# An adaLN, sliding-attention and SwiGLU kernel: chunk 0's softmax and attention output moved into the projection loop, loads of x and w_mod re-arranged

## The chip, the cores and the metric

The kernel runs on one core of a Trainium2 chip. Its time is the device time of one execution in microseconds. Where a text names an engine: TensorE (PE in the profile, PEld its weight loads), VectorE (DVE), ScalarE (ACT), GpSimd (POOL) and SyncE (SP), which here only issues DMAs.

## The reference

2048 tokens of width 576 (bf16) pass a modulated layer norm, attention of 32 heads of 18 over 8 earlier positions at distance 0, 2, ..., 14, a second modulated layer norm and a SwiGLU of width 4608.

```python
mod = (_silu(c) @ w_mod).reshape(c.shape[0], 6, 1, -1)      # sa, ca, ga, sb, cb, gb
h = _layernorm(x, axis=-1) * (1 + ca) + sa
x = x + ga * _A_ref(h, A_wqkv, A_wo)
h = _layernorm(x, axis=-1) * (1 + cb) + sb
x = x + gb * _B_ref(h, B_w1, B_w3, B_w2)
...
off = jnp.arange(W) * dil                                   # W, dil = 8, 2
idx = pos[:, None] - off[None, :]
mask = idx >= 0
logits = jnp.einsum('bhsd,bhswd->bhsw', q, kg) * scale      # kg = k[idx], vg = v[idx]
logits = jnp.where(mask[None, None, :, :], logits, -1000000000.0)
attn = _softmax(logits, axis=-1)
o = jnp.einsum('bhsw,bhswd->bhsd', attn, vg)                # then @ wo
...
h = _silu(x @ w1) * (x @ w3)                                # then @ w2
```

## The kernel before

Activations are held transposed, features on partitions and tokens in columns, in four chunks of 512 tokens.

**Prologue (L137 to L251).** 16 tiles of x are loaded through three buffers (`xst`, L139), alternately by SP and ACT, transposed on TensorE into `xT` and copied out by VectorE and ScalarE in turn. Then `w_mod` and `c` are loaded by GpSimd (L159 to L170) into a pool (`modp`) opened after `xst` is closed, so that it takes the same space. 150 small matmuls (L189) make the six modulation vectors `modT`. The indicator matrices `ind` and `indT4m` (which sum 18 features to a head, and spread a head's weight over its features) are built here too. `wqkv_sb` is loaded into the space of `modp` when that is released.

**Phase 1 (L280 to L344).** For each chunk n: the layer norm of chunk n+1 (`layer_norm_cols`, L91: statistics by matmuls with ones, then for five feature tiles a triple of VectorE operations: subtract L124, scale L128, shift L133), 75 matmuls for q, k and v (`pp`, L294 and L307, evacuated by ScalarE), and for each of the 8 distances j five products q*k on VectorE (`prod`, L324), five matmuls that sum them to heads (`lp`, L333) and a scaled copy to `lsb` (L339). A DMA puts the chunk's logits into `Lr` as rows 32n to 32n+31 (L342).

**Softmax (L348 to L387).** `Lr` is [128, 8, 512]: four chunks of 32 heads on partitions. One pass over it for all chunks: max over j, subtract, Exp on ScalarE, sum, reciprocal, product to `A_all`.

**Units (`emit_o_units`, L410).** A chunk has 40 units, five feature tiles by 8 distances: a matmul spreads the weights to the features (`aexp_ps`, L418), ScalarE copies them to bf16 (`aexp`, L425), VectorE multiplies with the shifted v (`tj`, L433) and adds to `oT` (L436).

**Head of a chunk (`head_of_chunk`, L444).** Projection by `wo`, gated residual into `xT` (L458), LN2 into `h2T`.

**Sweeps (L470 and L521).** Sweep a: for 36 tiles f of the hidden width load `w1c` and `w3c`, five matmuls for `up` and five for `gate`, a sigmoid on ScalarE, two products on VectorE to `hsw`; the units of the next chunk are spread over its tiles. Sweep b: 36 x 5 matmuls with `w2_sb`, residual, and transposes to the output.

The sequence of the main program is: phase 1 for four chunks, softmax, `w2_sb` load (L395, L396, into the space of the tiles before it), units and head of chunk 0, then for each chunk sweep a, head of the next chunk, sweep b.

A scheduler of the framework simulates the program and sets each engine's queue by program order and readiness; every engine then works through its queue in order. Pools are taken from two ends of the memory (`side="right"` and left) like stacks, so that a tile in re-used space waits for the last users of that space. The number of buffers of a pool sets how far a loop runs ahead.

## Time and profile before

| | us |
|---|---|
| median of 6 runs | 848.15 |
| lowest and highest | 845.93, 850.33 |
| profiled execution | 850.33 |
| its span | 848.5 |
| PE busy | 745.9 (88% of the span) |
| DVE busy | 512.1 (60%) |
| ACT busy | 299.7 (35%) |
| POOL busy | 81.0 (10%) |

The span is what the profiler saw, from the first to the last instruction; 1.8 us of the execution lie outside it. The shares are means over stages that have different limits, so they are read by stretches of time: prologue to about 52 us, phase 1 to 201.6, softmax to 233, units and head of chunk 0 with the first units of chunk 1 to about 296, sweeps to the end. A granted clock of 1.00 is 2.4 GHz, 0.50 is 1.2 GHz.

### The profile page before, as it was taken

The page shows a single profiled execution, that of the slowest core. Times are in us where ns is not written, and L with a number is a line of the kernel's source. Part 1 is how long each engine was busy: PE and PEld are TensorE (multiplying, and loading weights), DVE is VectorE, ACT ScalarE, POOL GpSimd, SP SyncE. Part 2 cuts the span into 40 slices and gives each one's busy share as a digit, 9 for nine tenths or more (in the row PEclk, how much of TensorE's full clock was granted, in tenths as well). Part 3 has the DMA queues.
Part 4 walks back from the last instruction along what each step waited for, and adds up shares of the span by engine and source line. Part 5 has one row for each costly group of instructions (what it writes and reads, how often), then busy time and mean ns, then how long its engine had stood idle before and what let it go on. Part 6 is the DMA issues. An engine that isn't in the chain of part 4 may idle for free.

```text
span 848.5 us, 11370 instructions
## 1 busy us (share of the span) xinstructions
PE 745.9 (88%) x3275; PEld 315.5 (37%) x3275; DVE 512.1 (60%) x1058; ACT 299.7 (35%) x521; POOL 81.0 (10%) x381
## 2 busy tenths in 40 slices
...
GB/s 135 196 103 0 1 25 25 1 25 67 0 250 1 21 95 111 111 89 109 7 76 110 109 112 92 8 29 134 112 108 111 35 15 98 113 112 112 42 1 28
DMA packets 185281, 62.15 MB, mean 73 GB/s; under 512 B 176068, under 2 KB 183428, under 8 KB 185092
## 3 DMA queue, kind: packets, MB, share of 16 engines
...
q10 hardware_dynamic: 91940, 27.10, 13.6%
...
q8 instruction: 26, 0.43, 0.2%
...
## 4 chain that ended last, share of the span: by engine, by line
PE 49%; DVE 12%; issue 9%; ACT 4%; DMA 2%; POOL 0%; ACTq 0%; POOLq 0%; DVEq 0%
PE gate_ps L504 18%; PE up_ps L497 13%; PE out_ps L529 10%; PE aexp_ps L418 3%; PE pp L452 2%; DVE g L512 2%; ACT sig L510 2%; DMA w1c<-in_B_w_dram 1%; DVE t L128 1%; DVE tj L433 1%; DVE t L124 1%; ACT aexp L425 1%; DVE h2T_new L133 1%; DVE oT_next L436 1%; DVE oT_cur L436 1%
## 5 line engine op out<-in xcount | busy, mean ns | idle before, releaser
L504 PE MATMUL gate_ps<-h2T_new,w1c 128*128 128x512 bf16 x720 | 182.4, 380 | 7.7 <-DVE g L512 4.0
L497 PE MATMUL up_ps<-h2T_new,w3c 128*128 128x512 bf16 x720 | 183.9, 382 | 2.9 <-DVE h2T_new L133 2.9
L510 ACT ACTIVATE sig<-gate_ps 128x512 bf16<-128x512 f32 x144 | 86.1, 598 | 263.3 <-PE gate_ps L504 244.8
L529 PE MATMUL out_ps<-hsw,w_sb 128*128 128x512 bf16 (+1 forms) x720 | 173.0, 382 | 6.8 <-DVE xT L535 4.5
L512 DVE TENSOR_TENSOR g<-gate_ps,sig 128x512 bf16<-128x512 f32 x144 | 99.3, 689 | 98.3 <-ACT sig L510 97.8
L425 ACT CAST aexp<-aexp_ps 126x512 bf16<-126x512 f32 (+1 forms) x160 | 88.0, 585 | 68.7 <-PE aexp_ps L418 37.7
L504 PEld LDWEIGHTS <-w1c 128*128 128x128 bf16 x720 | 69.0, 97 | 106.8 <-issue 39.0
L529 PEld LDWEIGHTS <-w_sb 128*128 128x128 bf16 (+1 forms) x720 | 72.1, 101 | 94.1 <-issue 16.0
L515 DVE TENSOR_TENSOR hsw<-g,up_ps 128x512 bf16<-128x512 bf16 x144 | 98.5, 685 | 9.1 <-PE out_ps L529 1.0
L497 PEld LDWEIGHTS <-w3c 128*128 128x128 bf16 x720 | 70.1, 98 | 84.5 <-issue 3.8
L418 PE MATMUL aexp_ps<-A_all,indT4m 128*126 128x512 bf16 (+1 forms) x160 | 60.6, 426 | 42.5 <-DVE A_all L384 31.2
L535 DVE SCALAR_TENSOR_TENSOR xT<-out_ps,modT,xT 128x512 bf16<-128x512 f32 (+1 forms) x20 | 14.9, 747 | 106.5 <-PE out_ps L529 106.5
L324 DVE TENSOR_TENSOR prod<-qT,kT 128x512 bf16<-128x512 bf16 (+11 forms) x160 | 57.1, 414 | 23.0 <-PE lp L333 11.7
L294 PE MATMUL pp<-hT_n,wqkv_sb 128*128 128x512 bf16 (+3 forms) x200 | 58.0, 398 | 4.8 <-DVE hT_n L133 3.6
L433 DVE TENSOR_TENSOR tj<-aexp,vT 126x512 bf16<-126x512 bf16 (+10 forms) x140 | 57.4, 418 | 3.4 <-ACT aexp L425 2.4
L493 POOL MEMSET w3c<- 64x128 bf16 x144 | 28.7, 200 | 262.9 <-PE up_ps L497 233.8
L494 POOL MEMSET w1c<- 64x128 bf16 x144 | 29.6, 206 | 253.6 <-PE gate_ps L504 189.3
L333 PE MATMUL lp<-prod,ind 128*32 128x512 bf16 (+1 forms) x160 | 47.4, 383 | 0.0
L418 PEld LDWEIGHTS <-indT4m 128*126 128x126 bf16 (+1 forms) x160 | 22.7, 144 | 65.9 <-issue 55.7
L436 DVE TENSOR_TENSOR oT_next<-oT_next,tj 126x512 bf16<-126x512 bf16 (+1 forms) x105 | 44.0, 419 | 1.5
L95 ACT ACTIVATE sq_t<-xT 128x512 bf16<-128x512 bf16 (+1 forms) x40 | 24.2, 627 | 32.3 <-PE stat_ps L109 24.4
L294 PEld LDWEIGHTS <-wqkv_sb 128*128 128x128 bf16 (+3 forms) x200 | 17.8, 101 | 45.3 <-issue 37.8
...
## 6 DMA issues: line engine op xcount, KB each, us to landing
...
wmod_sb<-in_w_mod_dram POOLq DMA_DIRECT2D x1, 3456.0 KB, 13.6
...
out_dram<-ob POOLq DMA_DIRECT2D x16, 144.0 KB, 2.3
```

Of the source, the lines that this page charges most:

```text
L294: nc.tensor.matmul(pp[0:orows, :], lhsT=wqkv_sb[0:krows, kc, col0:col0 + orows], rhs=hT_c[0:krows, kc, :], start=(kc == 0), stop=(kc == NS ...
L324: nc.vector.tensor_tensor(out=prod[0:rows, fc, lo:TC], in0=qT[0:rows, fc, s0 + lo:s0 + TC], in1=kT[0:rows, fc, s0 + lo - sh:s0 + TC - sh], ...
L418: nc.tensor.matmul(aexp_ps[0:rows, :], lhsT=indT4m[:, cc, fc, 0:rows], rhs=A_all[:, j, :], start=True, stop=True,)
L425: nc.scalar.copy(aexp[0:rows, :], aexp_ps[0:rows, :])
L433: nc.vector.tensor_tensor(out=tj[0:rows, lo:TC], in0=aexp[0:rows, lo:TC], in1=vsrc, op=ALU.mult)
L436: nc.vector.tensor_tensor(out=oT_c[0:rows, fc, lo:TC], in0=oT_c[0:rows, fc, lo:TC], in1=tj[0:rows, lo:TC], op=ALU.add,)
L497: nc.tensor.matmul(up_ps[:, :], lhsT=w3c[:, kc, :], rhs=h2T_c[:, kc, :], start=(kc == 0), stop=(kc == NSC - 1),)
L504: nc.tensor.matmul(gate_ps[:, :], lhsT=w1c[:, kc, :], rhs=h2T_c[:, kc, :], start=(kc == 0), stop=(kc == NSC - 1),)
L510: nc.scalar.activation(out=sig[:, :], in_=gate_ps[:, :], func=AF.Sigmoid)
L512: nc.vector.tensor_tensor(out=g2[:, :], in0=gate_ps[:, :], in1=sig[:, :], op=ALU.mult)
L515: nc.vector.tensor_tensor(out=hsw[:, f, :], in0=g2[:, :], in1=up_ps[:, :], op=ALU.mult)
L529: nc.tensor.matmul(out_ps[0:orows, :], lhsT=w2_sb[:, f, col0:col0 + orows], rhs=hsw[:, f, :], start=(f == 0), stop=(f == NF - 1),)
```

## The change

1. **Prologue.** `xst` has 16 buffers and SP issues all x loads at the start. The pool of `wmod_sb` and `cT` is opened before that of x, so it has space of its own. The loads of `cT` stand first on GpSimd, before the identity matrix is built. Two one-element copies from the 12th x tile into `wmod_sb` stand before its load, which by that is issued after that tile has landed.
2. **Chunk 0's softmax by itself.** After chunk 0's logits, four DMAs put them in `L0` as [128, 8, 128], four groups of 128 tokens on partitions, and a softmax of a quarter of the width gives `A0`; it is written in phase 1, before chunk 1's part. The big softmax follows after phase 1 as before, for chunks 1 to 3 (rows 0 to 31 of `Lr` are zeros), and its logits are now bf16.
3. **Chunk 0's units in phase 1.** 20 are written into the part of n=2 and 20 into that of n=3, each with four matmuls of 128 columns from `A0` in place of one of 512 from `A_all`.
4. **Buffers.** `p1ps` 4 to 3, `lps` 3 to 2, `hp` 3 to 2, `qT` per chunk (2) in place of whole, `aexp` and `tj` 3 to 2 (pool `ostg`), two PSUM banks for `aexp` during phase 1; later `ps_up` 3 to 2 and `ps_misc` 1 to 2.

TensorE's queue has 240 rows more, 120 matmuls and 120 loads. Between the last `lp` and the second `gate` of the first sweep stand 88 matmuls of units and 28 of projections by `wo` before the change, and 3 and 25 after it. From that gate on stand 2410 matmuls before and 2447 after; 29 of the 37 more are of units.

```diff
+    ostg = ctx.enter_context(tc.tile_pool(name="ostg", bufs=2, side="right"))
+    modp = tc.alloc_tile_pool(name="modp", bufs=1, side="right")
+    wmod_sb = modp.tile([128, NSC, 6 * D], BF16)
+    cT = modp.tile([128, NSC, 1], BF16)
+    for kc in range(NSC):
...
+        nc.gpsimd.dma_start(
+            cT[0:rows, kc, :],
...
+            if cc == 0:
+                for sub in range(NSUB):
+                    nc.tensor.matmul(
+                        aexp_ps[0:rows, sub * SUB:(sub + 1) * SUB],
+                        lhsT=indT4m[:, sub, fc, 0:rows],
+                        rhs=A0[:, j, :],
+                        start=True, stop=True,
+                    )
...
+    def softmax8(Lt, dstA, T, pool):
+        m4 = pool.tile([128, 4, T], F32, tag="m4")
+        nc.vector.tensor_tensor(out=m4[:, :, :], in0=Lt[:, 0:4, :], in1=Lt[:, 4:8, :], op=ALU.max)
...
+        Eb = pool.tile([128, NJ, T], BF16, tag="Eb")
+        nc.scalar.activation(out=Eb[:, :, :], in_=Lt[:, :, :], func=AF.Exp)
...
+        nc.vector.tensor_tensor(
+            out=dstA[:, :, :], in0=Eb[:, :, :],
+            in1=rsum[:, None, :].to_broadcast((128, NJ, T)), op=ALU.mult,
+        )
...
+        ps_aexp = pro.enter_context(tc.tile_pool(name="ps_aexp_pro", bufs=2, space=bass.MemoryType.PSUM))
...
-            xst = p0x.enter_context(tc.tile_pool(name="xst", bufs=3, side="right"))
+            xst = p0x.enter_context(tc.tile_pool(name="xst", bufs=16, side="right"))
...
+            for ti in range(NTOK128):
+                xs = xst.tile([128, D], BF16, tag="xs")
+                nc.sync.dma_start(xs[:, :], x2d[ti * 128:(ti + 1) * 128, :])
+                xs_all.append(xs)
+            nc.gpsimd.tensor_copy(wmod_sb[0:1, 0, 0:1], xs_all[11][0:1, 0:1])
+            nc.gpsimd.tensor_copy(wmod_sb[0:1, 4, 0:1], xs_all[11][0:1, 0:1])
+            nc.gpsimd.dma_start(
+                wmod_sb[:, 0:4, :], w_mod[0:512, :].rearrange("(kc p) o -> p kc o", p=128)
+            )
...
-                DMAQ[ti % 2].dma_start(xs[:, :], x2d[tsl, :])
...
-        Lr = att.tile([128, NJ, TC], F32)
-        hp = tc.alloc_tile_pool(name="hp", bufs=3, side="right")
+        Lr = att.tile([128, NJ, TC], BF16)
+        L0 = att.tile([128, NJ, SUB], BF16)
+        hp = tc.alloc_tile_pool(name="hp", bufs=2, side="right")
...
+        o0_parts = split_units(all_units(), NCH - 2)
...
-            p1ps = pps.enter_context(tc.tile_pool(name="p1ps", bufs=4, space=bass.MemoryType.PSUM))
-            lps = pps.enter_context(tc.tile_pool(name="lps", bufs=3, space=bass.MemoryType.PSUM))
+            p1ps = pps.enter_context(tc.tile_pool(name="p1ps", bufs=3, space=bass.MemoryType.PSUM))
+            lps = pps.enter_context(tc.tile_pool(name="lps", bufs=2, space=bass.MemoryType.PSUM))
...
+                if n >= 2:
+                    emit_o_units(0, oT0, o0_parts[n - 2], ps_aexp)
...
+                if n == 0:
+                    for sub in range(NSUB):
+                        DMAQ[sub % 2].dma_start(
+                            L0[32 * sub:32 * (sub + 1), :, :],
+                            lsb[0:H, :, sub * SUB:(sub + 1) * SUB],
+                        )
...
+                        softmax8(L0, A0, SUB, smp)
+                else:
+                    DMAQ[n % 2].dma_start(
+                        Lr[32 * n:32 * (n + 1), :, :], lsb[0:H, :, :]
+                    )
...
-    aexpp = ctx.enter_context(tc.tile_pool(name="aexpp", bufs=3, side="right"))
-    tjp = ctx.enter_context(tc.tile_pool(name="tjp", bufs=3, side="right"))
...
-    ps_up = ctx.enter_context(tc.tile_pool(name="ps_up", bufs=3, space=bass.MemoryType.PSUM))
+    ps_up = ctx.enter_context(tc.tile_pool(name="ps_up", bufs=2, space=bass.MemoryType.PSUM))
...
-    ps_misc = ctx.enter_context(tc.tile_pool(name="ps_misc", bufs=1, space=bass.MemoryType.PSUM))
+    ps_misc = ctx.enter_context(tc.tile_pool(name="ps_misc", bufs=2, space=bass.MemoryType.PSUM))
...
-    emit_o_units(0, oT_cur, all_units())
+    oT_cur = oT0
```

The first place is GpSimd's queue in the prologue, from the identity matrix to the small loads (`PE_49` and the like are the semaphores waited for; DMAHW ones are completion counters of DMAs). Before:

```order
masks.py:197 MEMSET ident 128x128
L245 MEMSET indT4m 128x2560
masks.py:199 ISA
masks.py:199 AFFINE_SELECT ident<-ident 128x128 [waits Pool_49]
L159 DMA wmod_sb<-in_w_mod_dram 128x4x3456 [waits DMAHW4_49,DMAHW3_49,DMAHW5_49,DMAHW2_49,DMAHW6_49,DMAHW1_49,DMAHW7_49,DMAHW0_49,PE_49]
L162 DMA wmod_sb<-in_w_mod_dram 64x3456
L167 DMA cT<-in_c_dram 128x1 x4
L167 DMA cT<-in_c_dram 64x1
```

After:

```order
L95 DMA cT<-in_c_dram 128x1 x4
L95 DMA cT<-in_c_dram 64x1
masks.py:197 MEMSET ident 128x128
L102 MEMSET sq_t 64x512 [waits Pool_49]
masks.py:199 ISA
masks.py:199 AFFINE_SELECT ident<-ident 128x128 [waits Pool_49]
L246 COPY wmod_sb<-xs 1x1 [waits DMAHW0_49]
L247 COPY wmod_sb<-xs 1x1
L297 MEMSET ind_f_576 128x160
L248 DMA wmod_sb<-in_w_mod_dram 128x4x3456 [waits Pool_49]
L251 DMA wmod_sb<-in_w_mod_dram 64x3456 [waits Pool_49]
```

The loads of `cT` moved to the front, and the load of `wmod_sb` waits, through the copy, for one x load instead of for TensorE's transposes and every x load. On SP the 16 x loads stand in a row, each from the fifth on with a wait for one of the eight DMA counters, which the five `wo_sb` loads use as well; on VectorE the casts of `cT` and the products with the sigmoid now stand ahead of the first copy to `xT`.

The second place is VectorE's queue in chunk 2's part of phase 1, the end of the layer norm of chunk 3 (`hT_n`) among the products. Before:

```order
L133 TENSOR_SCALAR hT_n_1263<-t_1296,modT_64 128x512 [waits DVE_49]
L324 TENSOR_TENSOR prod_1414<-qT_647,kT_648 64x512 [waits Activation_49]
L124 TENSOR_TENSOR t_1300<-xT_58,mean_t_77 128x512 [waits DVE_49]
L324 TENSOR_TENSOR prod_1427<-qT_647,kT_648 128x512
L128 SCALAR_TENSOR_TENSOR t_1300<-t_1300,onepca_65,rstd_t_78 128x512 [waits DVE_49]
L324 TENSOR_TENSOR prod_1427<-qT_647,kT_648 128x512
L133 TENSOR_SCALAR hT_n_1263<-t_1300,modT_64 128x512 [waits DVE_49]
L324 TENSOR_TENSOR prod_1427<-qT_647,kT_648 128x512
L124 TENSOR_TENSOR t_1304<-xT_58,mean_t_77 64x512 [waits DVE_49]
L324 TENSOR_TENSOR prod_1427<-qT_647,kT_648 64x512
L128 SCALAR_TENSOR_TENSOR t_1304<-t_1304,onepca_65,rstd_t_78 64x512 [waits DVE_49]
L133 TENSOR_SCALAR hT_n_1263<-t_1304,modT_64 64x512 [waits DVE_49]
```

After:

```order
L430 TENSOR_TENSOR prod_1674<-qT_1360,kT_661 128x512
L142 TENSOR_TENSOR t_1352<-xT_58,mean_t_81 128x512 [waits DVE_49]
L430 TENSOR_TENSOR prod_1674<-qT_1360,kT_661 128x512
L146 SCALAR_TENSOR_TENSOR t_1352<-t_1352,onepca_65,rstd_t_82 128x512 [waits DVE_49]
L187 TENSOR_TENSOR tj_1491<-aexp_1489,vT_73 126x508 [waits Activation_49]
L151 TENSOR_SCALAR hT_n_1315<-t_1352,modT_64 128x512 [waits DVE_49]
L190 TENSOR_TENSOR oT0_107<-oT0_107,tj_1491 126x508 [waits DVE_49]
L142 TENSOR_TENSOR t_1356<-xT_58,mean_t_81 64x512 [waits DVE_49]
L187 TENSOR_TENSOR tj_1501<-aexp_1499,vT_73 126x506 [waits Activation_49]
L146 SCALAR_TENSOR_TENSOR t_1356<-t_1356,onepca_65,rstd_t_82 64x512 [waits DVE_49]
L190 TENSOR_TENSOR oT0_107<-oT0_107,tj_1501 126x506 [waits DVE_49]
L151 TENSOR_SCALAR hT_n_1315<-t_1356,modT_64 64x512 [waits DVE_49]
```

Units of chunk 0 (`tj`, `oT0`) now stand among the operations of the layer norm and the products; each `tj` waits for a copy by ScalarE (`Activation_49`), which follows the unit's matmuls.

The third place is VectorE's queue after the last `prod` of phase 1: residual (`xT<-pp`), LN2 (`mean_t`, `var`, `t`) and softmax (`m`, `mx`, `Lr`, `s`). Before, the softmax stood alone, and the first unit followed it:

```order
L324 TENSOR_TENSOR prod<-qT,kT 128x512 x4
L324 TENSOR_TENSOR prod<-qT,kT 64x512
L353 TENSOR_TENSOR m_1746<-Lr 128x2048
L357 TENSOR_TENSOR m_1748<-m_1746 128x1024
L361 TENSOR_TENSOR mx<-m_1748 128x512
L364 TENSOR_TENSOR Lr<-Lr,mx 128x4096
L371 TENSOR_TENSOR s_1755<-Eb 128x2048
L375 TENSOR_TENSOR s_1757<-s_1755 128x1024
L379 TENSOR_TENSOR ssum<-s_1757 128x512
L383 RECIPROCAL rsum<-ssum 128x512
L384 TENSOR_TENSOR A_all<-Eb,rsum 128x4096
```

After:

```order
L504 SCALAR_TENSOR_TENSOR xT<-pp,modT,xT 128x512 x4
L211 TENSOR_TENSOR m_2183<-Lr 128x2048
L504 SCALAR_TENSOR_TENSOR xT<-pp,modT,xT 64x512
L213 TENSOR_TENSOR m_2185<-m_2183 128x1024
L120 TENSOR_SCALAR mean_t<-stat_2277 128x512
L215 TENSOR_TENSOR mx<-m_2185 128x512
L122 TENSOR_TENSOR msq<-mean_t 128x512
L216 TENSOR_TENSOR Lr<-Lr,mx 128x4096
L132 SCALAR_TENSOR_TENSOR var<-stat_2277,msq 128x512
L142 TENSOR_TENSOR t<-xT,mean_t 128x512
L136 TENSOR_SCALAR var<-var 128x512
L223 TENSOR_TENSOR s_2192<-Eb 128x2048
```

The residuals and LN2 of chunk 0 moved ahead of and in between the operations of the softmax; `A_all` stands after the first triple of LN2, and the other four triples follow it.

## Rows read from the trace of the kernel before

**Rows 1.** Busy time by stretch: us, then busy (instructions) PE, PEld, DVE, ACT, POOL; PEclk, DMA share, GB/s

```profile
124.20:158.20 34.00, 34.00 (x126) 10.95 (x125) 25.42 (x67) 16.84 (x27) 0.00 (x0) 1.00 0.08 16
158.20:189.60 31.40, 31.40 (x116) 10.07 (x115) 14.05 (x40) 13.33 (x23) 0.00 (x0) 1.00 0.08 18
189.60:201.60 12.00, 12.00 (x41) 3.11 (x40) 10.14 (x30) 4.69 (x8) 0.14 (x1) 1.00 0.00 1
201.60:233.00 31.40, 0.19 (x2) 0.22 (x2) 20.62 (x9) 4.20 (x2) 1.69 (x8) 0.52 0.23 45
233.00:266.00 33.00, 27.08 (x63) 9.60 (x63) 30.69 (x89) 27.68 (x51) 0.00 (x0) 0.68 0.46 161
266.00:293.00 27.00, 18.30 (x64) 6.97 (x62) 25.47 (x61) 17.36 (x29) 0.00 (x0) 0.94 0.00 1
...
296.50:438.00 141.50, 140.68 (x627) 61.64 (x626) 86.51 (x155) 45.10 (x73) 16.79 (x77) 0.98 0.36 81
```

**Rows 2.** The chain that ended last, in order of time: start, us, what

```profile
202.41 5.66 issue
...
212.38 4.44 DVE Lr L364
...
228.24 4.44 DVE A_all L384
...
291.56 0.66 DVE t L128
...
296.55 2.29 PE gate_ps L504 x5
```

**Rows 3.** Timeline of the prologue: start, us, engine, line, operation, count [idle before <-releaser]

```profile
17.70 2.80 PE L149 MATMUL pt<-ident,xs 128*128 128x128 bf16 x15
...
24.00 0.90 POOL L159 DMA_DIRECT2D wmod_sb<-in_w_mod_dram  x1 [20.49 <-PE pt L149]
...
39.40 0.15 DVE L176 CAST cTf<-cT 128x1 f32<-128x1 bf16 x1 [15.75 <-DMA cT<-in_c_dram]
...
42.41 9.74 PE L189 MATMUL pm_t<-silc,wmod_sb 64*128 64x1 bf16 x142
...
52.40 2.40 PE L98 MATMUL stat_ps<-xT,ones 128*128 128x512 bf16 x5 [0.25 <-DVE modT L196]
```

**Rows 4.** DMA issues from 0 to 60 us: KB each, us to landing

```profile
wmod_sb<-in_w_mod_dram POOLq DMA_DIRECT2D x1, 3456.0 KB, 13.6
...
xs<-in_A_x_dram SPq DMA_DIRECT2D x8, 144.0 KB, 2.3
```

**Rows 5.** Timeline of chunk 3's logits in phase 1

```profile
189.64 11.96 PE L333 MATMUL lp<-prod,ind 128*32 128x512 bf16 x40
...
191.03 10.14 DVE L324 TENSOR_TENSOR prod<-qT,kT 128x512 bf16<-128x512 bf16 x30 [6.69 <-PE lp L333]
```

**Rows 6.** Timeline of the output transposes at the end

```profile
840.52 0.52 PE L547 MATMUL pt<-ident,xT 128*128 128x128 bf16 x5 [0.55 <-DVE ob L551]
```

**Rows 7.** Groups by line and shape, weight loads: busy us, mean ns | idle

```profile
L418 PEld LDWEIGHTS <-indT4m 128*126 128x126 bf16 x128 | 18.8, 149 | 59.8 <-issue 52.1
```

**Rows 8.** Groups by line and shape, from 201 to 300 us

```profile
L425 ACT CAST aexp<-aexp_ps 126x512 bf16<-126x512 f32 x63 | 35.0, 585 | 24.9 <-PE aexp_ps L418 17.5 <-DVE tj L433 4.1 <-DVE oT_next L428 1.4
...
L458 DVE SCALAR_TENSOR_TENSOR xT<-pp,modT,xT 128x512 bf16<-128x512 f32 x4 | 3.0, 751 | 1.0 <-PE pp L452 1.0
L128 DVE SCALAR_TENSOR_TENSOR t<-t,onepcb,rstd_t 128x512 f32<-128x512 f32 x4 | 3.0, 746 | 1.1 <-ACT rstd_t L120 1.1
L124 DVE TENSOR_TENSOR t<-xT,mean_t 128x512 f32<-128x512 bf16 x4 | 2.7, 684 | 0.0
...
L133 DVE TENSOR_SCALAR h2T_new<-t,modT 128x512 bf16<-128x512 f32 x4 | 1.9, 478 | 0.0
```

**Rows 9.** Busy time by stretch within chunk 0's units, columns as in rows 1

```profile
237.00:241.00 4.00, 3.45 (x8) 1.20 (x7) 3.95 (x13) 3.32 (x7) 0.00 (x0) 0.50 1.08 392
...
255.00:260.00 5.00, 4.43 (x9) 1.45 (x9) 5.00 (x16) 4.34 (x8) 0.00 (x0) 0.50 0.00 0
```

200 lines of the change are left out of this document (92 added, 108 removed).

## The prediction

> **What bounds the kernel now.** I read three views in turn. The first is the table of busy time by stretch [rows 1], cut where the stages change. From 124.2 to 201.6 us (the rest of phase 1: the projections and logits of the four chunks) TensorE is busy all the time, 34.00 of 34.00, 31.40 of 31.40 and 12.00 of 12.00, while VectorE has 27.8 us free (8.6, 17.3 and 1.9). From 201.6 to 233 TensorE does 0.19 us of work. From 233 to 293 VectorE is the busiest engine (30.69 of 33, 25.47 of 27) and TensorE runs at a granted clock between its two levels, 0.68, so at 1.2 GHz for most of it. From 296.5 on TensorE has 0.8 us free in 141.5.
>
> The second view is the chain that ended last [rows 2]: after the last logits come 5.66 us for the DMA of `Lr`, then the softmax alone, which ends with `A_all` at 228.24 + 4.44 = 232.7, then units and head of chunk 0 until the last LN2 triple begins its product at 291.56, and the second `gate` of the first sweep at 296.55. The stretch from the end of the last `lp`, 189.64 + 11.96 = 201.6 [rows 5], to that gate is thus **94.9 us** with little TensorE work in it; the change aims there.
>
> The third view is the timeline of the prologue [rows 3]: `wmod_sb` is requested at 24.00, after 20.49 us of waiting for the last transposes; the first cast of `cT` starts at 39.40, the matmuls of the modulation run until 52.15, the first statistics start at 52.40.
>
> **Part 1, the prologue.** The request for `wmod_sb` no longer waits for the transposes but for the 12th of 16 x loads. An x load lands 2.3 us after its issue [rows 4]; all 16 now go through SP, and each waits for one of eight completion counters, shared with the `wo_sb` loads. I put the 12th at 10 us (an estimate: three rounds of landings at 2.3 each and some issue time; 7 if they stream, 14 if every round is held up). The load itself landed 13.6 us after issue [rows 4]; it now shares the DMA engines with the last four x tiles, so I take 14.6, landing at 24.6. The transposes take 2.8 us for three tiles [rows 3], 15 us for 16, and start near 6.5 since the casts of `cT` now stand in front of the `xT` copies on VectorE (the order shown with the change): they end near 21.5 and are hidden. The casts and sigmoids are hidden with them. The modulation is 150 pairs at 9.74/142 = 0.069 us [rows 3], 10.3. So the statistics of LN1 start at about 25.0 + 10.3 + 0.7 = 36.0 in place of 52.4: **-16.4** (-12 to -19). The `wqkv_sb` load still starts with the release of that space, as before, hidden behind LN1.
>
> **Part 2, chunk 0's units in phase 1.** On TensorE 160 matmuls of 128 columns with 160 loads replace 40 of 512 columns that stood after phase 1. No row shows this pair. Lower bound: five transposes of 128x128 in the tail took 0.52 us, 0.104 a pair [rows 6]; upper bound: a load of 128x126 of the same tile took 0.149 [rows 7] if nothing overlaps it. I take 0.12, nearer the first since loads overlap matmuls where TensorE has a queue of work: 19.2 us (16.6 to 23.8). TensorE is full there [rows 1], so all of this is on the path. VectorE gets 75 operations of 512 columns; 30 products took 10.14, 0.338 each [rows 5], so 25.4, and the small softmax, a quarter of the 20.62 [rows 1], 5.2 more. That is 30.6 against 27.8 free, and the free time isn't where the units are. Stage by stage:
> - n=0 and n=1: one bank less for `pp`, one less for `lp`, and the small softmax in front of LN1's triples: +4.5 (0 to 7).
> - n=2, from the end of its projections of `v` to the end of those of n=3: 72 pairs at 0.12, 40 matmuls of `lp` at 11.96/40 = 0.30 [rows 5] and 75 projections at 31.40/116 = 0.27 [rows 1] give 41; with LN1 of chunk 3 late (its operations stand behind a unit's product, in the order shown) I take 43.7 in place of 31.4: +12.3.
> - n=3: 40 `lp` took 12.0 [rows 5]. Now VectorE has 39 operations of units and 10 products (49 x 0.338 = 16.6), held up by the round trips through ScalarE to 20, then 20 more products, 6.8, and the last `lp`: 28, so +16.
>
> Sum **+32.8**; +22 if only TensorE's share and 3 of the first stage count, +45 if the round trips cost half again as much.
>
> **Part 3, from the last `lp` to the gate.** The units are gone from here; `wo`, the residual and LN2 of chunk 0 are interleaved with the softmax of chunks 1 to 3 on VectorE, whose queue decides (the order shown). The softmax stays at 20.6 [rows 1]: the bf16 `Lr` does not make it faster, as `A_all` with bf16 in and out took 4.44 like `Lr` in f32, 4.44 [rows 2]. Five residuals at 0.75, five triples at 0.75 + 0.68 + 0.48 [rows 8], and four operations of statistics at 0.69 or less, 2.3 in all, give 36.2. Waiting: TensorE makes the five projections of `wo` at 5 x 0.27 each, slower than the residuals take them (2.9), Exp stands between subtraction and sum (1.9), and Ln and Exp of LN2 stand behind it on ScalarE (1.5). That is 42; the gate follows 3.6 later, as now (the last triple, 291.56 + 0.75 + 0.48, ends near 292.9). The chunk's DMA, 5.66 before [rows 2], is hidden behind the projections. So 94.9 becomes 45.6: **-49.3** (-45 to -53).
>
> **Part 4, after the gate.** By the order, 37 matmuls (29 of them units of chunk 1) that lay before that gate now lie behind it, where TensorE is full: 140.68/627 = 0.22 each [rows 1], +8. `w2_sb` is still requested after `A_all`, but that is now five us before the sweep begins, not sixty. In the trace it drew 392 GB/s with the DMA engines full [rows 9], beside a demand of 81 GB/s in the sweep [rows 1]: w1 and w3 have three buffers each of lead; I take +1 (0 to 6). The Trainium skill, "DMA: Bandwidth & Descriptors", section "Issuing engines are not separate DMA queues", says that transfers of all issuing engines run on the same 16 DMA engines and interleave, which speaks against this place; by it the tiles of the first sweep would come at a share of the rate for some 15 us, and the sum would go by the 6. No row of before has the two together. Two banks for `up` in place of three: 0 (to +4; the gate's bank is single anyway), a second bank for the output transposes: -0.5. Sum **+8.5** (0 to 14).
>
> **Sum.** -16.4 + 32.8 - 49.3 + 8.5 = -24.4. The profiled execution took 850.33 (1.8 of it outside the span, taken as it is), which is 2.2 above the median of its runs: 825.9 by it, **823.7** by the median.
>
> **The rivals.**
> - *The units are hidden better.* If VectorE takes them in its free time and phase 1 grows by TensorE's 19.2 and 3 only, the sum is -35: 813. For it: the 17.3 us free in n=2. Against: the units' chain PE, ScalarE, VectorE has two buffers at each step.
> - *The clock falls in n=2 and n=3.* From 237 to 241 and from 255 to 260, in the units of before, TensorE was 86 and 89% busy and yet granted 0.50, that is 1.2 GHz [rows 9]; there it waited for ScalarE between pairs of matmuls. If that comes with the units, some 115 large matmuls cost 3.45/8 = 0.43 [rows 9] in place of 0.28 for part of the time, about +14: 838. Against: from 124.2 to 201.6 the clock is 1.00 [rows 1], and `lp` and `pp` fill the waits. The Trainium skill, "TensorE: Matmul & The Clock Gate", section "Part 1: The HAM clock gate", states that the throttled clock is the default and that activity releases it; by that the busy phase 1 would keep the full clock and the sum stays, by the rows it need not.
> - *`wmod_sb` comes late.* If SP's x loads take until 18, part 1 gives 8: 832.
> - *Nothing is left.* If part 2 costs 45 and parts 1 and 4 stand at their bad ends, the sum is near zero: 848.
> - *Slower.* One loop: a unit's four matmuls need an `aexp` bank, which ScalarE frees with a copy of 0.585 [rows 8], whose target VectorE frees, and TensorE's queue is in order, so `lp` behind a waiting unit waits too. If a round takes 4 x 0.12 + 0.585 + 2 x 0.338, about 1.75, and nothing else fits in, 40 rounds cost 70 in place of the 28.3 of n=2 and n=3: 865. It decides from a round of (28.3 + 24.4)/40, about 1.3 us, on. Against it: two buffers let the steps of neighbouring units overlap, and with three, from 233 to 266, ScalarE was busy 27.68 of 33 [rows 1].
>
> **How the numbers follow.** Forecast 0.55 (812 to 836), better hidden 0.15, lower clock 0.10, late `wmod_sb` 0.05, nothing left 0.05, slower 0.10. A measurement can tell about 0.3%, 2.5 us, from no change. Faster: 0.55 + 0.15 + 0.10 + 0.05 = 0.85; same 0.05; slower 0.10. The range leaves out the last two and the tail of the better case: 805 to 842.
>
> **What would show it.** Right: the statistics of LN1(0) start near 36; the last `lp` ends 16 us later than now (201.6 - 16.4 + 32.8 = 218); the second gate 45 us behind it, near 264; the first sweep pair ends 8 later relative to its gate. Wrong: a granted clock below 1 before the last `lp`; DMA as the releaser of `gate` or `up` in the first ten tiles; `aexp` waiting for ScalarE more than 1 us a unit; the statistics of LN1 after 44.

## The result, and the profile after

| kernel | median us | runs | lowest to highest | ratio to before, 95% interval |
|---|---|---|---|---|
| before | 848.51 | 16 | 845.93 to 851.16 | |
| after | **822.98** | 8 | 819.54 to 825.08 | **0.9694** (0.9677 to 0.971) |

The change saves 25.5 us; forecast were 823.7, with 805 to 842 as the range. The profiled execution of after took 825.14, with a span of 823.4 against 848.5 before, 25.1 less. One execution of the kernel with the units behind the loop (below) took 4003.36 us, almost five times its other three; it is left out there. The profile shows where each part of the sum came out:

| stretch | before | after | difference | forecast |
|---|---|---|---|---|
| start to the first LN1 statistics | 52.40 | 38.46 | -13.9 | -16.4 |
| from there to the end of the last `lp` | 149.2 | 174.4 | +25.2 | +32.8 |
| from there to the second `gate` of the first sweep | 94.95 | 44.57 | -50.4 | -49.3 |
| from there to the end of the span | 551.95 | 566.0 | +14.1 | +8.5 |
| sum | 848.5 | 823.4 | -25.0 | -24.4 |

The total was hit more closely than its parts: phase 1 cost 7.6 us less than forecast, the stretch behind the gate 5.6 more and the prologue gained 2.5 less. That these errors nearly cancel is luck.

**The prologue.** The timeline of after, with columns as in [rows 3] (start, us, engine, line, operation, count, and in brackets the idle time before and what ended it):

```profile
0.82 11.29 SPq L244 DMA_DIRECT2D xs<-in_A_x_dram  x16
...
5.36 0.59 PE L259 MATMUL pt<-ident,xs 128*128 128x128 bf16 x4 [5.36 <-POOL ident masks.py:199]
6.47 0.15 DVE L272 CAST cTf<-cT 128x1 f32<-128x1 bf16 x1 [5.33 <-DMA cT<-in_c_dram]
...
10.33 3.12 PE L259 MATMUL pt<-ident,xs 128*64 128x128 bf16 x18 [4.38 <-DVE xT L261]
...
12.81 0.18 POOL L246 COPY wmod_sb<-xs 1x1 bf16<-1x1 bf16 x1 [7.50 <-DMA xs<-in_A_x_dram]
...
13.28 0.77 POOL L248 DMA_DIRECT2D wmod_sb<-in_w_mod_dram  x1
...
38.46 1.86 PE L116 MATMUL stat_ps<-xT,ones 128*128 128x512 bf16 x4 [0.25 <-DVE modT L292]
```

The first matmul waits until 5.36 for `ident`, which POOL makes behind the requests for `cT`; the next large group waits 4.38 for an `xT` copy that stands behind the casts on VectorE; and the one-element copy that holds back `wmod_sb`, called its marker from here on, runs at 12.81, not at 10: its x tile has to come first.

**Phase 1, the head and the first sweep.** Busy time by stretch (columns as in [rows 1]). The first two rows answer to the rows of 158.20 and 189.60 of before, the next two to those from 201.60 to 293, the last to the one of 296.50:

```profile
149.50:187.40 37.90, 37.90 (x189) 15.37 (x188) 28.50 (x80) 22.61 (x41) 0.00 (x0) 1.00 0.04 8
187.40:212.80 25.40, 21.20 (x121) 9.90 (x121) 23.36 (x68) 15.29 (x28) 0.82 (x4) 0.87 0.00 1
212.80:239.00 26.20, 9.49 (x37) 3.40 (x37) 19.31 (x19) 11.17 (x11) 1.07 (x6) 0.70 0.20 44
239.00:257.40 18.40, 8.42 (x19) 2.61 (x19) 16.35 (x17) 2.79 (x4) 0.60 (x3) 0.50 0.44 152
257.40:277.40 20.00, 15.71 (x52) 6.36 (x51) 11.07 (x25) 6.45 (x14) 1.60 (x8) 0.75 0.72 200
277.40:410.00 132.60, 131.87 (x609) 59.27 (x608) 89.07 (x167) 49.05 (x82) 15.67 (x71) 1.00 0.35 78
```

The bound changes from row to row: TensorE in n = 2 (37.90 of 37.90), VectorE in n = 3 (23.36 of 25.40) and from the last `lp` to the gate (19.31 of 26.20, 16.35 of 18.40), TensorE again from 277 on. In between lies a stretch of 20 us in which TensorE is short by a fifth (15.71) and is granted 0.75. From TensorE's timeline of after, where it waits between the last `lp` and there:

```profile
206.39 6.43 PE L439 MATMUL lp<-prod,ind 128*32 128x512 bf16 x19 [0.29 <-DVE prod L430]
213.63 5.69 PE L498 MATMUL pp<-oT,wo_sb 126*128 126x512 bf16 x25 [0.81 <-ACT lsb L445]
...
238.99 0.58 PE L534 MATMUL up_ps<-h2T_new,w3c 128*128 128x512 bf16 x1 [13.01 <-DVE h2T_new L151]
...
248.36 0.59 PE L172 MATMUL aexp_ps<-A_all,indT4m 128*126 128x512 bf16 x1 [7.93 <-DVE A_all L230]
...
257.39 2.34 PE L541 MATMUL gate_ps<-h2T_new,w1c 128*128 128x512 bf16 x5
...
265.54 1.25 PE L534 MATMUL up_ps<-h2T_new,w3c 128*128 128x512 bf16 x5 [2.43 <-DMA w3c<-in_B_w_dram]
268.66 2.29 PE L541 MATMUL gate_ps<-h2T_new,w1c 128*128 128x512 bf16 x5 [1.86 <-DVE g L549]
```

Between `lp` and gate two waits on VectorE, 13.01 and 7.93, make up 21 of the 44.6 us. Behind the gate the first wait is for a DMA. On VectorE the softmax's two largest operations are as long as before, with the bf16 `Lr` as well ([rows 2] have 4.44 for both):

```profile
224.62 4.41 DVE L216 TENSOR_TENSOR Lr<-Lr,mx 128x4096 bf16<-128x4096 bf16 x1
...
243.89 4.42 DVE L230 TENSOR_TENSOR A_all<-Eb,rsum 128x4096 bf16<-128x4096 bf16 x1
```

### The profile page after: what moved, and what is told of

Read it like the earlier page. It is cut to its first block, busy times and chain, and to the rows that moved or that the text cites. A ratio compares the mean times of both kernels' runs of the same rounds, so it can differ in the third digit from the quotient of the medians.

```text
span 823.4 us, 11713 instructions
## 1 busy us (share of the span) xinstructions
PE 747.6 (91%) x3395; PEld 321.9 (39%) x3395; DVE 521.2 (63%) x1067; ACT 300.5 (36%) x523; POOL 85.2 (10%) x385
## 3 DMA queue, kind: packets, MB, share of 16 engines
q10 hardware_dynamic: 91332, 25.53, 13.2%
## 5 line engine op out<-in xcount | busy, mean ns | idle before, releaser
L534 PE MATMUL up_ps<-h2T_new,w3c 128*128 128x512 bf16 x720 | 186.1, 385 | 17.2 <-DVE h2T_new L151 14.5
L396 PE MATMUL pp<-hT_n,wqkv_sb 128*128 128x512 bf16 (+3 forms) x200 | 63.4, 412 | 5.2 <-DVE hT_n L151 4.8
L439 PE MATMUL lp<-prod,ind 128*32 128x512 bf16 (+1 forms) x160 | 52.1, 398 | 2.3 <-DVE prod L430 2.2
L172 PE MATMUL aexp_ps<-A_all,indT4m 128*126 128x512 bf16 (+1 forms) x120 | 38.2, 391 | 9.2 <-DVE A_all L230 7.9
L113 ACT ACTIVATE sq_t<-xT 128x512 bf16<-128x512 bf16 (+1 forms) x40 | 24.4, 628 | 41.5 <-DVE msq L122 17.7
L445 ACT ACTIVATE lsb<-lp 32x512 bf16<-32x512 f32 x32 | 18.7, 586 | 32.9 <-PE lp L439 32.8
## 6 DMA issues: line engine op xcount, KB each, us to landing
wmod_sb<-in_w_mod_dram POOLq DMA_DIRECT2D x1, 3456.0 KB, 13.5
```

Of the source, the lines that this page charges most:

```text
L396: nc.tensor.matmul(pp[0:orows, :], lhsT=wqkv_sb[0:krows, kc, col0:col0 + orows], rhs=hT_c[0:krows, kc, :], start=(kc == 0), stop=(kc == NS ...
L439: nc.tensor.matmul(lp[0:H, :], lhsT=ind[0:rows, fc, :], rhs=prod[0:rows, fc, :], start=(fc == 0), stop=(fc == NSC - 1),)
L534: nc.tensor.matmul(up_ps[:, :], lhsT=w3c[:, kc, :], rhs=h2T_c[:, kc, :], start=(kc == 0), stop=(kc == NSC - 1),)
```

## The experiments

The theory to be tested is the prediction's: the prologue's 14 us and the units' move are two gains that add; the units cost phase 1 less than they cost behind it, since VectorE has time free there; VectorE's queue decides from the last `lp` to the gate; `w2_sb` costs the first tiles. The rivals are in the expectations. A kernel's time is compared with runs of before on the same chip.

### The two gains apart

The kernel before with the change's prologue alone:

```diff
-            xst = p0x.enter_context(tc.tile_pool(name="xst", bufs=3, side="right"))
+            xst = p0x.enter_context(tc.tile_pool(name="xst", bufs=16, side="right"))
...
+                nc.sync.dma_start(xs[:, :], x2d[ti * 128:(ti + 1) * 128, :])
...
+            nc.gpsimd.tensor_copy(wmod_sb[0:1, 0, 0:1], xs_all[11][0:1, 0:1])
...
-                DMAQ[ti % 2].dma_start(xs[:, :], x2d[tsl, :])
...
```

> The kernel before with part 1 of the change alone (16 x buffers, all x loads on SP, c first, w_mod behind the 12th x tile). In the trace of the changed kernel the first statistics start 13.9 us earlier than before (38.46 against 52.40). If the parts add, as I think, this gives 848.5 - 13.9 = 834.6 and the statistics start at 38.5. If something later absorbs an earlier start (a wait for weights in phase 1), 838 to 848.

Measured: 835.32 us, ratio 0.9849 (0.9825 to 0.9874), with the statistics at 38.44. The changed kernel with the prologue of before (the same diff the other way):

> The changed kernel with the prologue of before. If the parts add: 823.0 + 13.9 = 836.9, statistics at 52.4, and from there on the same distances as in the changed kernel (174.4 us to the end of the last lp). If the parts share something, the sum of the two gains differs from 25.5 by more than 2 us.

Measured: 836.57 us, ratio 0.9871 (0.9844 to 0.9898), statistics at 52.54. So -12.2 for the prologue (847.50 to 835.32) and -10.9 for the rest; together -23.1 where the change brings -25.5. The gains add to within 2.4 us, about what these intervals can tell. The 14.0 by which the statistics start earlier lie within the interval of the prologue's 12.2 (10.7 to 14.8), so no loss of it on the way is seen.

### Why not 16 us in the prologue

`ident` made first, the casts of `cT` held until the tenth x tile has landed, `wmod_sb` asked for behind the eighth:

```diff
...
+    make_identity(nc, ident[:])
     for kc in range(NSC):
...
-            nc.gpsimd.tensor_copy(wmod_sb[0:1, 0, 0:1], xs_all[11][0:1, 0:1])
+            nc.gpsimd.tensor_copy(wmod_sb[0:1, 0, 0:1], xs_all[7][0:1, 0:1])
...
+            nc.gpsimd.tensor_copy(cTf[0:1, :, 0], xs_all[9][0:1, 0:NSC])
```

> The changed kernel with the identity matrix built ahead of the loads of c on GpSimd, the casts of c held back by a one-element copy until x tile 9 has landed, and w_mod behind x tile 7 in place of 11. In the trace of the changed kernel TensorE's first transpose waits 5.4 us for the identity matrix and 4.4 for copies that stand behind the casts, and w_mod is awaited for another 2.5 after the last transpose. Theory: the transposes end near 19 and w_mod lands near 23, so the first statistics start 3 to 5 us earlier than at 38.46 and the time is 818 to 820. Rival: w_mod and the x tiles share the DMA engines, and x lands later by as much: 822 to 824.

Measured: 823.34 us, ratio 0.9702 (0.9681 to 0.9722). A miss; the statistics start at 37.04, 1.4 earlier. Its TensorE timeline shows where the removed waits went:

```profile
3.77 1.45 PE L261 MATMUL pt<-ident,xs 128*128 128x128 bf16 x7 [3.77 <-DMA xs<-in_A_x_dram]
...
12.08 5.36 PE L261 MATMUL pt<-ident,xs 128*64 128x128 bf16 x28 [4.23 <-DVE cTf L273]
...
25.62 0.35 PE L286 MATMUL pm_t<-silc,wmod_sb 128*128 128x1 bf16 x8 [1.04 <-DMA wmod_sb<-in_w_mod_dram]
```

The wait for `ident` is gone, but the held casts hold the `xT` copies behind them on VectorE for 4.23 us, the same wait in another place. Neither wait sets the start of the statistics, though: in both kernels TensorE waits for `wmod_sb` at the end, 1.04 here and 2.46 in after. The modulation begins at 25.62 in place of 26.83 because the request for `wmod_sb` stands at 11.76 in place of 13.28. It gains no more since the marker of the eighth tile runs at 10.68, only 2.1 before that of the twelfth in after: the x tiles themselves come late. What would bring them earlier was not tried.

### What the place in the loop is worth, and what a pair costs

All 40 units written behind the loop in place of in its last two chunks:

```diff
-                if n >= 2:
-                    emit_o_units(0, oT0, o0_parts[n - 2], ps_aexp)
...
+        emit_o_units(0, oT0, all_units(), ps_aexp)
...
```

> The changed kernel with the 40 units of chunk 0 written after the projection loop in place of inside it; they use the small softmax as in the change. Theory: the loop gives back the 20 us that the units cost it, but VectorE then has 28 us of units and 20.6 of softmax one behind the other, without gaps, ahead of chunk 0's residual, so 828 to 836. Rival: it is the early small softmax that brings the gain, since units can fill the big softmax's gaps from then on, and the place inside the loop brings nothing: 820 to 825.

Measured: 831.66 us (the median of three), ratio 0.981 (0.978 to 0.9841). The last `lp` ends at 193.5, 19.3 earlier, but behind it TensorE has little to do:

```profile
193.10:230.00 36.90, 12.51 (x90) 10.15 (x90) 33.37 (x49) 15.39 (x23) 1.11 (x6) 0.56 0.15 31
```

12.51 of 36.90 at a granted clock of 0.56, for most of it the 1.2 GHz level, while VectorE is busy 33.37. So the place in the loop is worth some 9 us, and the units alone show the lower clock that [rows 9] show before.

Every pair of load and matmul of 128 columns issued twice (160 pairs more, no other engine gets more work):

```diff
-                for sub in range(NSUB):
+                for sub in [0, 0, 1, 1, 2, 2, 3, 3]:
```

> The changed kernel with each of the 160 matmuls of 128 columns of chunk 0's units issued twice, with its load: 160 pairs more. It measures the pair, which the prediction had put at 0.12 (bounds 0.104 and 0.149). The trace of the changed kernel shows four in 0.38 us from start to start, 0.095. Theory: in chunk 2's part TensorE is busy all the time, so 80 x 0.095 = 7.6 come on top there; in chunk 3's part TensorE has 4.2 of 25.4 us free, so 3 to 4 of the other 7.6: 823.0 + 11 = 834 (832 to 837). Rival: a pair costs its load of 0.149, then 842 or more; or the units are bound by ScalarE and VectorE in both parts, then 823 to 826.

Measured: 824.94 us, ratio 0.9728 (0.9712 to 0.9744): 2 us in place of some 11. A miss that names the mis-sized term. Two rows of its timeline, the same unit matmuls in runs of 16 and of 8:

```profile
166.27 1.08 PE L165 MATMUL aexp_ps<-A,indT4m 128*126 128x128 bf16 x16
168.25 0.67 PE L165 MATMUL aexp_ps<-A,indT4m 128*126 128x128 bf16 x8
```

Eight more pairs take 0.41 us, 0.051 each. By stages: n = 2 grows from 37.9 to 42.2, 4.3 for 80 pairs, 0.053 each. That figure is a little too low for a pair: in this run the pairs of two units stand side by side in n = 2, in runs of mostly 16, in after mostly in runs of 4, so that there are fewer runs as well. n = 3, also with 80 more, takes 25.2, in after 25.4: there they lie in TensorE's waits for VectorE.

30 of the units in n = 2 and 10 in n = 3:

```diff
-        o0_parts = split_units(all_units(), NCH - 2)
+        o0_parts = [all_units()[0:30], all_units()[30:40]]
```

> The changed kernel with 30 of chunk 0's units written in chunk 2's part of the loop and 10 in chunk 3's, in place of 20 and 20. Theory: chunk 2's part is bound by TensorE (44.40 of 44.40 busy, VectorE 9.9 free), chunk 3's by VectorE (23.4 of 25.4); ten units moved cost 40 x 0.095 = 3.8 in the first and save 10 x 2 x 0.338 = 6.8 in the second: -3, so 820. Rival: chunk 2's part turns VectorE-bound by the ten, or chunk 3's by TensorE: 822 to 825.

Measured: 818.99 us, ratio 0.9663 (0.9639 to 0.9686). From the end of the projections of `v` to the next such end n = 2 takes 41.3 (+3.4), and n = 3 takes 19.2 (-6.2). A unit costs 0.34 us where TensorE is the bound and 0.62 where VectorE is. That n = 3 is VectorE's stage is shown by both runs. The stages give a gain of 2.8 us over the change; by the ratios it is at the edge of what can be told, as the two intervals overlap.

### The 5 us of chunks 0 to 2

Phase 1 loses 5.2 us before any unit is in it. The kernel before with the smaller buffers alone:

```diff
...
-        hp = tc.alloc_tile_pool(name="hp", bufs=3, side="right")
+        hp = tc.alloc_tile_pool(name="hp", bufs=2, side="right")
...
-            p1ps = pps.enter_context(tc.tile_pool(name="p1ps", bufs=4, space=bass.MemoryType.PSUM))
-            lps = pps.enter_context(tc.tile_pool(name="lps", bufs=3, space=bass.MemoryType.PSUM))
+            p1ps = pps.enter_context(tc.tile_pool(name="p1ps", bufs=3, space=bass.MemoryType.PSUM))
+            lps = pps.enter_context(tc.tile_pool(name="lps", bufs=2, space=bass.MemoryType.PSUM))
```

(`hp` holds the normalized chunk; the expectation names it wrongly as the buffer of the products.)

> The kernel before, with the buffers of the changed kernel in phase 1 and nothing else of it: 3 instead of 4 PSUM buffers for q, k and v, 2 instead of 3 for the pairs' logits, 2 instead of 3 for the products. Asks where the 5.2 us come from by which the changed kernel is later at the end of chunk 2's v, before any unit stands in the loop. Theory (the smaller buffers make TensorE wait for evictions): 851 to 853, with the last pair of the loop 3 to 5 us later counted from the first statistics. Rival (buffers make no difference, and the 5.2 us are the extra matmuls of the merged chunk and the other orders): 847 to 849.

Measured: 852.16 us, ratio 1.0061 (1.0041 to 1.0081). The buffers cost 3.9 us in the median; in the trace the end of chunk 0's `v` is 1.7 later than in before, of chunk 1's 3.0, and from chunk 2's on 3.3, up to the last `lp`. Its first projections show how (the first row is of before, the other two are of this run):

```profile
66.19 1.86 PE L294 MATMUL pp<-hT_n,wqkv_sb 128*128 128x512 bf16 x4 [0.17 <-DVE hT_n L133]
...
64.18 1.44 PE L294 MATMUL pp<-hT_n,wqkv_sb 128*128 128x512 bf16 x3 [2.98 <-DVE hT_n L133]
66.22 1.44 PE L294 MATMUL pp<-hT_n,wqkv_sb 128*128 128x512 bf16 x3 [0.60 <-DVE hT_n L133]
```

With three banks three projections follow each other while LN1 makes the next row of `hT_n`, and TensorE waits 0.60; before, four did, and it waited 0.17. The changed kernel has the same rows (1.44, x3, 0.60). So 3.3 of the 5.2 are the price of the smaller buffers, of which the two PSUM banks went to the units' `aexp`. No run splits the other 1.9.

### `w2_sb` and the first sweep

`w2_sb` in four quarters behind the tiles f = 4, 7, 10 and 13 of the first sweep (f counts from 0), in place of two halves ahead of it:

```diff
-    nc.sync.dma_start(w2_sb[:, 0:NF // 2, :], B_w2[0:(NF // 2) * 128, :].rearrange("(f p) d -> p f d", p=128))
-    nc.scalar.dma_start(w2_sb[:, NF // 2:, :], B_w2[(NF // 2) * 128:, :].rearrange("(f p) d -> p f d", p=128))
...
+            if cc == 0 and f in W2_AT:
...
+                nc.gpsimd.tensor_copy(w2_sb[0:1, f0, 0:1], w1c[0:1, 0, 0:1])
+                DMAQ[p % 2].dma_start(
+                    w2_sb[:, f0:f1, :],
+                    B_w2[f0 * 128:f1 * 128, :].rearrange("(f p) d -> p f d", p=128),
+                )
```

> The changed kernel with the load of w2_sb cut in four and each quarter held back, by a one-element copy, until tile 4, 7, 10 or 13 of w1 in the first sweep has landed. Theory: what the stretch after the second gate lost beyond its 37 matmuls (6 us) is the w2_sb load, whose 390 GB/s hold back w1 and w3 and by the wait let the clock fall; then the waits for w3c and for the gate there go and the time is 817 to 819. Rival: the loss comes from two banks for up in place of three, or from the clock that is low there anyway; then 822 to 824.

Measured: 826.76 us, ratio 0.9756 (0.9729 to 0.9784): a miss. In 18 pieces of two tiles each, one behind each tile from f = 3 on (`p` from 0 to 17, otherwise the same diff):

> As the run with w2_sb in quarters, but in 18 pieces of 288 KB (two of the 36 tiles each), one behind each tile of w1 from the fourth on. In the run with quarters the second gate started at full clock and without a wait, yet 565.2 us followed it, against 566.0 in the changed kernel: each quarter held back w1 and w3 again (w1c took 5.5 us to land in place of 2.4). Theory: it is the size of the piece against the lead of three buffers that decides; pieces as small as a tile's own weights cause no wait, and the time is 817 to 820. Rival: the bytes themselves cost it, whatever their cut, or the loss does not come from w2_sb: 823 to 827.

Measured: 824.37 us, ratio 0.9715 (0.9703 to 0.9728): a miss too. The first 20 us behind the second gate in before, in these two (first w2_sb late, then in pieces), as one row of busy time each; the row of 257.40 above is that of after:

```profile
296.50:316.50 20.00, 19.95 (x80) 8.52 (x80) 16.13 (x33) 8.37 (x15) 2.39 (x12) 0.87 0.42 95
```

```profile
259.20:279.20 20.00, 18.06 (x81) 8.33 (x83) 15.72 (x33) 8.68 (x16) 2.75 (x14) 1.00 0.71 184
```

```profile
260.10:280.10 20.00, 19.00 (x79) 8.48 (x81) 15.65 (x33) 9.52 (x18) 3.69 (x18) 0.93 0.64 160
```

TensorE does 80 matmuls in before, 52 in after, and 81 and 79 in the two variants. So the loss of after in this stretch, 28 matmuls at 0.22 or 6.2 us, comes with `w2_sb`, which moved 390 GB/s from 257.4 to 262. In after a load of `w1c` asked for by SP landed 10.2 us after its issue, in before 2.4 (KB each and median us to landing, from 296 to 380 us in before and from 240 to 300 in after; not every load has a landing on record):

```profile
w1c<-in_B_w_dram SPq DMA_DIRECT2D x14, 128.0 KB, 2.4
...
w1c<-in_B_w_dram SPq DMA_DIRECT2D x7, 128.0 KB, 10.2
```

But the variants give most of the 6 us back. Their gates stand 46.9 and 46.7 us behind the last `lp` in place of 44.6, with 2.5 us of waiting for `g` just ahead (the expectation of the pieces says there was none), so the three are better counted from the end of the last `lp`, for 64.57 us and for the 130 us that follow (after, then w2_sb late, then in pieces; the second pair of figures in a row is TensorE's weight loads, one for each matmul, of which a few have no record):

```profile
212.82:277.39 64.57, 33.59 (x105) 12.35 (x105) 46.72 (x59) 20.40 (x28) 3.25 (x17) 0.66 0.43 123
277.39:407.39 130.00, 129.37 (x599) 58.15 (x598) 87.49 (x164) 47.50 (x79) 14.77 (x68) 1.00 0.34 76
...
212.32:276.89 64.57, 33.89 (x128) 14.00 (x131) 53.12 (x75) 25.26 (x35) 3.97 (x20) 0.76 0.28 68
276.89:406.89 130.00, 125.08 (x569) 55.92 (x579) 80.12 (x145) 42.20 (x71) 14.77 (x68) 1.00 0.44 106
...
213.39:277.96 64.57, 33.34 (x127) 13.77 (x130) 52.42 (x73) 24.84 (x35) 3.89 (x18) 0.76 0.27 64
277.96:407.96 130.00, 125.64 (x571) 56.63 (x582) 84.48 (x157) 45.38 (x77) 17.92 (x81) 1.00 0.45 107
```

The variants are 26 and 25 loads ahead of after at first (131 and 130 against 105), and 7 and 9 at the end (710 and 712 against 703), at 0.22 some 2 us. With the late quarters TensorE waits 4.7 us for DMAs behind the gate (2.9 for `w1c`, 1.4 for `w_sb`, 0.4 for `w3c`) and 6.3 for `g`; with the pieces 2.2 and 8.4; in after 2.8 and 2.7. (The waits are counted from 240 us on and hold the 2.5 us in front of the second gate in the two variants.) In all three the load is moved beside the stream of w1 and w3; in before it lay ahead of the gate, where that stream had not begun. Further on, a difference of 2 us between two traces says nothing; *What stays open* below shows why.

### The idle 21 us between `lp` and gate

If VectorE is the bound there, half of its work can be put elsewhere: the softmax of chunks 1 to 3 is computed in `A_all` itself in operations of 512 columns, maxima and subtractions ahead of LN2's triples, and sums, reciprocals and products in the first ten tiles of the first sweep, where a copy on POOL holds them back; the units of chunk 1 start behind these ten tiles. `hsw` is placed ahead of `w2_sb`, whose request then follows phase 1.

```diff
...
-        o0_parts = split_units(all_units(), NCH - 2)
+        o0_parts = [all_units()[0:30], all_units()[30:40]]
...
-            softmax8(Lr, A_all, TC, smp)
...
+            def sub(j=j):
+                nc.vector.tensor_tensor(out=A_all[:, j, :], in0=A_all[:, j, :], in1=sm_mx[:, :], op=ALU.subtract)
+                nc.scalar.activation(out=A_all[:, j, :], in_=A_all[:, j, :], func=AF.Exp)
...
+        if cc == 0:
+            steps = softmax_steps()
+            per_f = [[] for _ in range(U0)] + split_units(all_units(), NF - U0)
...
+            budget = 1.25
+            if steps and f == 0:
+                while len(steps) > NJ - 1 + 4 + NJ:
+                    steps.pop(0)[1]()
+                nc.gpsimd.tensor_copy(sm_s[0:1, 0:1], hsw[0:1, f, 0:1])
+            while steps and (budget > 0 or f == U0 - 1):
+                w, fn = steps.pop(0)
+                budget -= w
+                fn()
```

> Two edits to the changed kernel. The 40 units of chunk 0's first half stand 30 in the tiles of n = 2 and 10 in those of n = 3, as in the run with that split (818.99 us). And the softmax of chunks 1 to 3, which in the changed kernel stands whole ahead of the second LayerNorm, is cut: its maxima, subtractions and Exps are written ahead of LN2's last steps, and its sums, reciprocals and products are spread over the first ten tiles of the first feed-forward sweep, with the units of chunk 1 from the tenth tile on. Theory (VectorE holds TensorE between the last pair of the loop and the second gate: TensorE is busy about 18 of 44.6 us there, VectorE about 36): some 15 us of VectorE's work leave the path to the gate, so the gate stands some 28 to 32 us behind the last pair instead of 44.6, and with TensorE the bound of the sweep the time falls to 803 to 810. Rival (VectorE has no room in the first tiles of the sweep, where it already makes the gated product g): the gate comes earlier but the first tiles stretch by as much, TensorE waits for g, and the time stays at 815 to 820.

Measured: **807.37 us**, ratio 0.9524 (0.9505 to 0.9544), as the theory has it; the gate comes 0.6 us behind its range. Its TensorE timeline, and its busy time from the last `lp` to the gate and in the first 20 us behind it:

```profile
200.46 8.09 PE L439 MATMUL lp<-prod,ind 128*32 128x512 bf16 x24 [0.29 <-DVE prod L430]
...
229.29 0.58 PE L564 MATMUL up_ps<-h2T_new,w3c 128*128 128x512 bf16 x1 [10.79 <-DVE h2T_new L151]
...
241.17 2.29 PE L571 MATMUL gate_ps<-h2T_new,w1c 128*128 128x512 bf16 x5 [2.32 <-DVE g L579]
```

```profile
208.60:241.20 32.60, 15.51 (x50) 5.25 (x51) 21.68 (x40) 13.71 (x20) 1.61 (x8) 0.69 0.68 209
...
241.20:261.20 20.00, 19.33 (x76) 7.98 (x78) 18.33 (x29) 5.27 (x9) 2.76 (x14) 0.91 0.43 95
```

The gate stands 32.6 us behind the last `lp` (200.46 + 8.09 to 241.17) in place of 44.4 in the run with 30 and 10 units, and from it to the end it is 564.3 against 563.4: 11.8 gained, 0.9 given back. In the first tiles VectorE is busy for 18.33 of 20 us and TensorE for 19.33, with 76 matmuls where after has 52.

Two things moved in that run, the softmax (and with it the units of chunk 1, which need it) and `w2_sb`. To have the second alone, `hsw` was placed ahead of `w2_sb`, the logits collected in `A_all`, and the scratch of the softmax put where `hsw` lies later:

```diff
...
-        Lr = att.tile([128, NJ, TC], BF16)
+        Lr = A_all
...
-            smp = p2.enter_context(tc.tile_pool(name="sm", bufs=1, side="right"))
+            smp = p2.enter_context(tc.tile_pool(name="sm", bufs=1))
...
+    hsw = pleft.tile([128, NF, TC], BF16)
     w2_sb = pleft.tile([128, NF, D], BF16)
-    hsw = pleft.tile([128, NF, TC], BF16)
```

> The changed kernel with 30 units in n = 2 and 10 in n = 3 (818.99 us), and one thing more: w2_sb lies behind hsw in memory instead of ahead of it, the logits are collected in A_all itself and the softmax's scratch lies where hsw comes later, so that the request for w2_sb no longer has to wait for the softmax. The order of the instructions on every engine is unchanged. It takes apart the two edits of the run that took 807.37 us: this is the early w2_sb without the moved softmax. Theory (w2_sb's collision with the stream of w1 and w3 costs the first sweep 5 us net): the load is over before the second gate, TensorE waits less than 1 us for DMAs in the first ten tiles, and the time is 812 to 815. Rival (as w2_sb late and w2_sb in pieces suggested, taking the waits away gives nothing back): 817 to 820.

Measured: 817.62 us, ratio 0.9636 (0.961 to 0.9662). It decides nothing between the two, since the edit didn't bring the early request: it still came behind the last product of the softmax, as SyncE's row shows, 30.7 us later than in the kernel of 807.37 us (213.55).

```profile
244.24 0.37 SPq L478 DMA_DIRECT2D w_sb<-in_B_w_dram  x1
```

What it does show is that the other places in memory alone change nothing that can be told (817.62 against 818.99, with overlapping intervals). How the 11.6 us of the run before divide between the moved softmax and the early `w2_sb` stays open; the gate itself, 11.8 earlier, doesn't need `w2_sb`.

Last, the kernel of 807.37 us with all 40 units in n = 2:

```diff
-        o0_parts = [all_units()[0:30], all_units()[30:40]]
+        o0_parts = [all_units(), []]
```

> The kernel that took 807.37 us (softmax of chunks 1 to 3 behind LN2, its second half spread over the first tiles), with all 40 units of chunk 0's first half in the tiles of n = 2 and none in those of n = 3. Theory (n = 2 is bound by TensorE with room on VectorE, n = 3 by VectorE with room on TensorE): n = 2 grows by 3 to 4 as it did from 20 to 30 units, n = 3 shrinks from 19 to about 13, and the time is 803 to 806. Rival (at 40 units VectorE is full in n = 2 too, or the chain from TensorE through ScalarE to VectorE holds it up): n = 2 grows by 6 or more, and the time is 807 to 810.

Measured: **803.67 us**, ratio 0.9463 (0.9446 to 0.948), 19.3 less than the changed kernel. n = 2 and n = 3 in one row:

```profile
147.80:204.30 56.50, 56.48 (x307) 24.23 (x308) 51.83 (x148) 37.77 (x69) 0.85 (x4) 1.00 0.03 6
```

TensorE is busy for 56.48 of 56.50 at the full clock, VectorE for 51.83; after took 63.3 there, and 60.5 with 30 and 10. The sum is as the theory has it (57.7); its division isn't, since 15 `lp` matmuls of n = 2 now stand behind the `v` of n = 3, and "n = 2 grows by 3 to 4" can't be read off.

## Why the prediction was right, point by point

- **Prologue, -13.9 for -16.4.** The mechanism was right (`wmod_sb` asked for early, transposes hidden), the term too large by 2.5: the marker of the 12th x tile runs at 12.81 where 10 was taken. The 12.81 is within the bounds given (7 to 14). SP's x loads took 3.1 us to land in place of 2.3, and SP waited 3.3 us in all for the `wo_sb` loads, whose completion counters it shares; the prediction names the sharing and gives it no price of its own. The `wmod_sb` load itself then took 13.5 us where 14.6 was allowed. The wait for `ident` wasn't foreseen, but is hidden behind `wmod_sb`.
- **Units in phase 1, +25.2 for +32.8.** This step failed in size, in three places. For chunks 0 to 2 +5.2 for +4.5, of which the smaller buffers are 3.3. For n = 2 +6.5 for +12.3: the price of a pair, 0.12, was too high. What was measured lies below even the lower bound of 0.104, which was a run of five transposes divided by five. A short run holds a fixed share: 8 pairs take 0.67 and 16 take 1.08, so some 0.26 and 0.051 for each (for five that makes 0.51, and 0.52 was read). The doubled pairs cost 0.053 each in n = 2, with fewer and longer runs; with 40 units in a TensorE-bound n = 2, n = 2 and n = 3 take 56.5 in place of 43.3, 13.2 for 160 pairs, 0.083 each with the changes from one kind of matmul to the other. LN1 of chunk 3, late in the order, cost little: 72 pairs at 0.083 are 6.0 of the 6.5. For n = 3 +13.5 for +16: VectorE is the bound as taken, and the stage is 2.5 shorter than the 28 of the forecast.
- A figure on this: the Trainium skill, "TensorE: Matmul & The Clock Gate", section "Back-to-back issue gap", gives about 81 ns a matmul for a stream of loads and matmuls of 128 columns. The 0.083 here agree with it, the 0.051 of a pair more in a long run lie below it; by it the 19.2 of the prediction would have been an estimated 13.0.
- **Last `lp` to gate, -50.4 for -49.3.** Right in size and cause. The order of VectorE's queue, with durations from [rows 2] and [rows 8], gave 45.6 and the trace 44.6. That VectorE's queue decides is shown by the moved softmax: VectorE's busy time there fell from 35.7 (19.31 + 16.35) to 21.7, and the gate came 11.8 earlier. The units of chunk 1 left that stretch as well; their share was not measured.
- **Behind the gate, +14.1 for +8.5.** This step failed in size too. The 8 for the matmuls that moved behind the gate stand. `w2_sb` was taken at 1 with 6 as the upper end; the trace shows 28 matmuls too few in 20 us, 6.2, and 130 us later still 22 (649 weight loads since the gate where before has 671), 4.8: near the upper end. The reason given for 1, three buffers of lead on w1 and w3, was wrong: a load of `w1c` took 10.2 us to land. Two things add up in the first 20 us: 2.8 us of waits for DMAs, and behind them the clock. From the same table for after, cut finer:

```profile
262.00:267.00 5.00, 2.37 (x11) 0.87 (x9) 0.36 (x2) 0.00 (x0) 0.29 (x2) 1.00 1.07 257
267.00:272.00 5.00, 3.34 (x8) 1.29 (x8) 3.10 (x7) 2.57 (x6) 0.31 (x2) 0.56 0.43 95
```

  The clock had risen to 1.00; then TensorE was busy 2.37 of 5 us while the DMA engines were full, and in the next 5 us it was granted 0.56, mostly the 1.2 GHz level; over the 20 us 0.75, in before 0.87. The Trainium skill's section that the prediction weighed, "Issuing engines are not separate DMA queues" in "DMA: Bandwidth & Descriptors", says that the transfers of all issuing engines share the same DMA engines; the 10.2 us of this trace fit it, but don't prove it, since SP had asked for a half of `w2_sb` itself and its own order of transfers would do the same.
- **The rivals.** *Better hidden* (813): phase 1 went some 70% of the way from the forecast's 32.8 to its 22.2. *The clock falls in n = 2 and n = 3*: in n = 2 it stayed at 1.00; in n = 3 it was 0.87, in TensorE's waits for VectorE, where 80 more pairs cost nothing either. *`wmod_sb` late* and *nothing left* didn't come. *Slower* by the units' round trips: a unit costs 0.34 to 0.62, far from the 1.3 from which it decides.

The signs seen beforehand: statistics near 36 (38.5), the last `lp` 16 later (11.2), the gate 45 behind it (44.6), DMA as releaser of `up` or `gate` in the first tiles as a sign against (it came, 2.43 and 0.4), and a granted clock below 1 before the last `lp` as another (it came too, 0.87 in n = 3).

**What stays open.** From the last `lp` to the end of the span, kernels with the same code there differ by up to 5.4 us: 606.4 with the prologue of before, 607.4 with doubled pairs, 607.9 with 30 and 10 units, 610.6 in after, 611.8 with the other prologue. Their traces show where much of it lies: in one stage some 560 us behind the last `lp`. Two stretches of 10 us each, in after and then in the run with 30 and 10 units, both from 555 us behind the last `lp` on:

```profile
767.82:777.82 10.00, 6.94 (x29) 2.75 (x28) 4.95 (x8) 1.79 (x3) 0.00 (x0) 0.92 0.00 0
777.82:787.82 10.00, 10.00 (x36) 3.97 (x35) 0.00 (x0) 0.00 (x0) 0.00 (x0) 0.74 0.01 2
...
762.52:772.52 10.00, 6.94 (x31) 2.82 (x30) 5.11 (x8) 1.79 (x3) 0.00 (x0) 1.00 0.00 1
772.52:782.52 10.00, 9.22 (x45) 4.21 (x44) 0.75 (x1) 0.00 (x0) 0.00 (x0) 1.00 0.01 2
```

TensorE is busy for 6.94 of 10 us in both; then the clock is 0.74 in one and stays at 1.00 in the other, and in the 20 us TensorE starts 63 weight loads against 74, at 0.22 some 2.4 of the 2.7 us between these two kernels. What decides which way it goes isn't known. The statistics start between 37.4 and 40.5 with the same prologue. So a difference of 2 us between two of these single traces isn't read as an effect. Whether `w2_sb` ahead of the gate alone would bring back what it costs behind it is not settled.
